# Remainder weight rows: two 64-row transfers for two groups each, in place of one mirrored 128-row transfer

## The chip, the cores and the metric

The kernel runs on one core of a Trainium2 chip. TensorE (PE) multiplies matrices, VectorE (DVE) and ScalarE (ACT) work on elements and empty PSUM, GpSimd (POOL) does small element work and issues some transfers, and SyncE (SP) issues all the others. Each engine executes its own list of instructions in order and waits on semaphores. Sixteen DMA engines move the data. The metric is device time in microseconds of one launch; smaller is better.

## The reference, cut to what matters

```python
x = A_x                                # 1 x 2048 x 576, bf16
xn = layernorm(x)
qkv = xn @ wqkv                        # 576 x 1728; 32 heads of 18
scores = q @ k.T * 18 ** -0.5          # causal, window of 256 keys
s = (softmax(scores) @ v) @ wo         # 576 x 576
h = sigmoid(xn @ w_gate) * (xn @ w_up) # 576 x 4608 each
g = silu(h @ w_down)                   # 4608 x 576
out = x + s * g
```

The contraction length that matters here is 576 = 64 + 4 x 128. PE's array is used as two tiles of 64 rows each, so a matrix with 576 rows makes four blocks of 128 rows and a remainder of 64 rows.

## The kernel before, in words

The 2048 tokens are worked off in four chunks of 512. For each chunk the kernel makes the layer norm, the transposed normalized input `xnT`, the projections to Q, K and V, the windowed attention of 8 groups of 4 heads, the output projection, and the feed-forward part: 36 tiles `ft` of 128 hidden columns, each with a gate and an up matrix (`gate_up`, line 881), a tanh on ACT (line 904), a multiplication on DVE into `hT` (line 907), and then the down projection (`down`, line 944).

All work is first written as a graph of operations with dependencies and priorities. `schedule` (line 1030) is a planner: with estimated durations, it places one operation after another on the five engines, which fixes each engine's list and which PSUM slot an operation gets. `emit` (line 1124) writes the lists out, with waits on semaphores. A change to a transfer's estimated bytes or count can therefore reorder everything that is planned later. The feed-forward matmuls of chunk 0 begin first, ahead of attention, split by token blocks (`PARTS`) as `xnT` becomes ready; warm-up matmuls on zeros (line 424) fill PE before that and end when the planner places the first gate/up matmul.

`turn` (line 102) and `pair` (line 94) issue the matmuls of one product. In `pair`, output 0 is computed with rows 0 to 63 of the array (`ROWS[0]`, the first row tile), output 1 with rows 64 to 127. With a block of 128 weight rows, each of the two outputs needs both halves, so it is run twice with the halves swapped. The remainder block k = 0 is run only once: output 0 takes its 64 remainder weight rows from partitions 0 to 63, output 1 from partitions 64 to 127.

For the weights this means: `load_nat` (line 399) loads the four blocks of 128 rows in one transfer. `load_rem` (line 403) loads the remainder of 64 rows for two matrices (or two halves of one matrix) in one transfer that fills 128 partitions. Its source access pattern has three dimensions, the outermost of size 2:

```python
return self.dma(dst, bass.AP(a.tensor, a.offset, [(step, 2), a.ap[0], (1, n)]), P * n * 2, ...)
```

It is used for Q and K (`wqkr`), for the two column halves of V (`wvr`) and of the output matrix (`wor`). Gate and up are different tensors, so one transfer can't take both. Therefore `weights` (line 843), which loads the groups of two `ft` tiles for chunk 0, mirrors: one transfer brings the gate rows of group g to partitions 0 to 63 and those of group g + 1 to 64 to 127, another the up rows of group g + 1 to partitions 0 to 63 and those of group g + 2 to 64 to 127. In odd groups gate and up have then changed sides, and `gate_up` swaps them (`flip`, line 885), with their PSUM banks. The first up group and the last one are loaded alone, as transfers of 64 rows. The remainder of all 18 groups stays in `wgr` for the later chunks; the four blocks are loaded again in each chunk, through a ring of 4 group slots in `wgs`.

All these loads are in SP's list, in the planner's order. In the first chunk it begins with `x`, the gate and up loads of groups 0 to 3 with their remainders, `wqk`, `wqkr`, `wv`, `wvr`; later loads wait for slots that PE releases. `xr` is the input of the next chunk's layer norm; its statistics (lines 480, 482) and the copies of Q and K columns (`wq4`, lines 439 and 443, which wait for all of `wqk` and `wqkr`) stand in DVE's list between the multiplications for `hT`.

The softmax here doesn't subtract the row's maximum and nothing guards it: scores larger than these inputs give would overflow.

## Time and profile before

| | us |
|---|---|
| median of 8 runs | 584.12 |
| lowest, highest | 582.87, 585.42 |
| profiled execution, own time | 584.22 |
| its span in the profile | 582.4 |
| PE busy | 569.1 (98%) |
| DVE busy | 346.5 (60%) |
| ACT busy | 268.9 (46%) |
| POOL busy | 180.1 (31%) |
| SP waits for PE, total of 63 waits | 215.3 |

The profile is of one execution. Its span runs from the first to the last instruction; the measured time includes what lies around. Busy times are per engine, and engines work beside each other, so that they don't add up. PE's granted clock is full throughout. 62.05 MB are moved in 105748 packets, at 107 GB/s in the mean; in the first 50 us it is about 200 GB/s. In rows of the profile, `out<-in` gives the tiles that an instruction writes and reads, and brackets give the idle time before it and what ended it.

### The profile page before, as it was taken

The numbers are of one execution on the slowest core, as the hardware profiler recorded it, in microseconds if no ns is written. First come the engines' busy times: TensorE is split into PE (matmuls) and PEld (weight loads), VectorE is DVE, ScalarE is ACT, GpSimd is POOL, SyncE is SP. The second block draws the span as 40 slices with busy tenths as digits, with TensorE's granted clock in tenths as the row PEclk, the third lists the DMA queues.
The fourth block names the chain that finished last, engine by engine and source line by source line (L and its number), as shares of the span: only waits on it lengthen the run. The fifth ranks groups of instructions, "written<-read, shape, count | busy, mean of one in ns | idle before, by whom it ended". The sixth has DMA issues, their size and how long they took to land.

```text
span 582.4 us, 21466 instructions
## 1 busy us (share of the span) xinstructions
PE 569.1 (98%) x9536; PEld 356.7 (61%) x9536; DVE 346.5 (60%) x837; ACT 268.9 (46%) x379; POOL 180.1 (31%) x290
## 2 busy tenths in 40 slices
PE   7998999999999999999999999999999999999996
PEld 5554555597785555555677865555457754444786
DVE  4358989856789974677877476777431133333123
ACT  2245576534366844765743654867220023333111
POOL 7454465334457522145355215630000000000000
PEclk9999999999999999999999999999999999999999
DMA  6677899743213333243412003533350014442010
GB/s 178 202 216 229 202 221 195 208 99 64 61 41 105 104 113 100 74 119 101 99 37 54 25 24 95 155 111 110 109 146 20 25 58 137 140 144 73 2 43 23
DMA packets 105748, 62.05 MB, mean 107 GB/s; under 512 B 14996, under 2 KB 104292, under 8 KB 105656
## 3 DMA queue, kind: packets, MB, share of 16 engines
q1 hardware_dynamic: 100536, 55.95, 35.7%
q0 software_dynamic: 5120, 4.74, 3.4%
q8 instruction: 75, 1.23, 0.9%
q14 instruction: 17, 0.14, 0.1%
HBM read 51.61 MB, written 2.36 MB: 93 GB/s over the span
## 4 chain that ended last, share of the span: by engine, by line
PE 90%; DMA 3%; SPq 3%; DVE 2%; issue 1%; ACT 1%; DVEq 0%
PE ps L98 90%; SPq L254 3%; DMA xr<-in_A_x_dram 2%; DMA wqkr<-in_A_wqkv_dram 1%; DVE hT L907 1%; ACT tring L904 1%; PE ps L550 0%; DVE s_attn L1011 0%; DVE thf L1016 0%; DVE wq L443 0%; DVE xf L1021 0%; DVE expr L714 0%; DVE small L482 0%; DVE wq L439 0%; DVE mask L461 0%
## 5 line engine op out<-in xcount | busy, mean ns | idle before, releaser
L98 PE MATMUL ps<-xnT,wgs 64*128 64x512 bf16 (+2 forms) x2400 | 288.9, 368 | 0.4 <-issue 0.3
L701 ACT ACTIVATE expr<-ps 128x1024 bf16<-128x1024 f32 (+2 forms) x160 | 156.5, 983 | 67.4 <-PE ps L98 66.4
L98 PEld LDWEIGHTS ps<-xnT,wgs 64*128 64x128 bf16 x2400 | 111.5, 94 | 113.6 <-PE ps L98 2.3
L98 PE MATMUL ps<-wd_sb,hT 64*128 64x288 bf16 (+2 forms) x2448 | 155.6, 276 | 0.0
L907 DVE SCALAR_TENSOR_TENSOR hT<-tring,ps 128x512 bf16<-128x512 bf16 x144 | 98.7, 686 | 78.4 <-ACT tring L904 71.7
L904 ACT ACTIVATE tring<-ps 128x512 bf16<-128x512 f32 x144 | 85.8, 596 | 128.0 <-PE ps L98 126.8
L98 PEld LDWEIGHTS ps<-wd_sb,hT 64*128 64x128 bf16 x2448 | 114.2, 94 | 26.0
L254 POOL DMA_DIRECT2D qk<-qd x160 | 82.3, 523 | 85.2 <-DVE qd L588 33.2
L666 POOL TENSOR_SCALAR kx<-kprev,small 128x256 bf16<-128x256 bf16 x64 | 64.4, 1016 | 85.4 <-PE ps L98 85.0
L714 DVE TENSOR_TENSOR expr<-expr,mask 128x256 bf16<-128x256 bf16 (+2 forms) x232 | 65.9, 306 | 37.7 <-ACT expr L701 36.3
L98 PE MATMUL ps<-xnT,wgr 64*128 64x512 bf16 (+2 forms) x300 | 56.0, 368 | 5.6 <-DVE hT L907 3.4
L98 PE MATMUL ps<-qk,kx 64*128 64x320 bf16 (+4 forms) x736 | 59.7, 251 | 0.0
L767 DVE TENSOR_REDUCE pvs<-ps 64x304 f32<-64x608 f32 x64 | 50.4, 788 | 15.2 <-PE ps L98 13.8
L98 PEld LDWEIGHTS ps<-qk,kx 64*128 64x128 bf16 x736 | 31.7, 94 | 26.2 <-ACT expr L701 1.0
L1001 ACT ACTIVATE thf<-ps 128x576 bf16<-128x576 f32 (+3 forms) x22 | 11.4, 520 | 61.1 <-PE ps L98 60.6
L98 PEld LDWEIGHTS ps<-v_aug,expr 64*128 64x128 bf16 x2432 | 35.4, 93 | 6.0
L98 PE MATMUL ps<-v_aug,expr 64*128 64x19 bf16 (+1 forms) x2432 | 35.8, 170 | 0.0
L98 PE MATMUL ps<-xnT,wqk 64*128 64x512 bf16 x256 | 32.6, 375 | 0.0
L1004 DVE SCALAR_TENSOR_TENSOR thf<-thf,ps 128x576 bf16<-128x576 bf16 x12 | 9.0, 753 | 30.0 <-ACT thf L1001 29.4
L98 PEld LDWEIGHTS ps<-xnT,wgr 64*128 64x128 bf16 x300 | 15.0, 94 | 18.8 <-DVE hT L907 5.0
L666 DVE TENSOR_SCALAR kx<-qk,small 128x512 bf16<-128x512 bf16 x64 | 23.6, 393 | 1.9 <-PE ps L98 1.6
L588 DVE CAST qd<-ps 128x1024 bf16<-128x1024 f32 (+1 forms) x20 | 22.2, 1115 | 3.8 <-PE ps L98 3.3
(66 smaller groups left out, 292.1 us busy)
## 6 DMA issues: line engine op xcount, KB each, us to landing
wgs<-in_B_w_gate_dram SPq DMA_DIRECT2D x72, 256.0 KB, 3.1
wgs<-in_B_w_up_dram SPq DMA_DIRECT2D x72, 256.0 KB, 3.5
wd_sb<-in_B_w_down_dram SPq DMA_DIRECT2D x9, 576.0 KB, 6.7
qk<-qd POOLq DMA_DIRECT2D x100, 36.0 KB, 2.0
xf<-in_A_x_dram SPq DMA_DIRECT2D x16, 144.0 KB, 2.2
out_dram<-xf SPq DMA_DIRECT2D x16, 144.0 KB, 1.8
xr<-in_A_x_dram SPq DMA_DIRECT2D x6, 288.0 KB, 3.9
wqk<-in_A_wqkv_dram SPq DMA_DIRECT2D x2, 576.0 KB, 6.5
```

The costliest lines, as they stand in the source:

```text
L98: res = eng.matmul(outs[i], lhs(ROWS[t], i), rhs(ROWS[t], i), start=start, stop=stop, tile_position=(64 * t, 0))
L254: o = self.op(eng, DMA_ISSUE_NS[eng], lambda e: e.dma_start(dst, src), name, deps, prio, nbytes=nbytes)
L588: return eng.tensor_copy(dst, self.both(h, n))
L666: return e.tensor_scalar(self.kx[:, sx, pos:pos + n_ // SW, t, :], src.rearrange("p (s k) -> p s k", k=SW), self.half[:, t:t + 1], None, A ...
L701: return eng.activation(self.expr[:, se, :, lo * SW:NT], self.both(h, NT)[:, :, lo * SW:NT], ACTF.Exp, scale=SM_SCALE)
L714: return eng.tensor_tensor(e_, e_, m_, ALU.mult)
L767: return eng.tensor_reduce(out[ROWS[i]], src, mybir.AxisListType.X, ALU.add)
L904: th = op("ACT", act_ns(NT), lambda e: e.activation(self.tring[:, st, :], bank(h, 0), ACTF.Tanh, scale=0.5), f"th:{c}:{ft}", deps=[pg, dt_ ...
L907: mu = op("DVE", dve_ns(NT), lambda e: e.scalar_tensor_tensor(self.hT[:, ft, :], self.tring[:, st, :], 1.0, bank(h, 1), ALU.add, ALU.mult) ...
L1001: return e.activation(v2(t)[:, a:b, :], y2()[:, a:b, :], ACTF.Tanh, scale=0.25)
L1004: q1 = op("DVE", dve_ns(w), lambda e: e.scalar_tensor_tensor(v2(t), v2(t), 1.0, y2(), ALU.add, ALU.mult), f"fq1:{nm}", deps=[th, f2], prio=0)
```

## The change

`load_rem` now takes a list of sources and makes one transfer of 64 rows for each: the first to partitions 0 to 63, the second to 64 to 127, each on a semaphore of its own. Q and K, the halves of V and the halves of the output matrix so have two transfers instead of one. For gate and up, each even group loads the gate rows of itself and of the next group (512 columns) to the first row tile, and the up rows of the same two groups to the second. No group is mirrored: `flip` goes, and `wgr` shrinks from two slots of 2560 columns to one of 4608. The `wgr` transfers are 18 of 64 KB, where there were 17 of 64 KB and 2 of 32 KB. The planner's estimated bytes for a transfer of 64 rows are set to 1.5 times its real bytes, as they were for the two transfers of 64 rows before.

```diff
-        self.wgr, _ = seq("wgr", [P, 2, F // 2 + WG * P])
+        self.wgr, _ = seq("wgr", [P, F])
...
-    def load_rem(self, dst, src, step, n, name, lane, prio, deps=()):
-        a = src[0:RD, 0:n]
-        return self.dma(dst, bass.AP(a.tensor, a.offset, [(step, 2), a.ap[0], (1, n)]), P * n * 2, name, lane, deps=deps, prio=prio)
+    def load_rem(self, dst, srcs, name, lane, prio, deps=()):
+        return [self.dma(dst[ROWS[t], :], src[0:RD, :], RD * src.shape[1] * 3, name, lane + (t,), deps=deps, prio=prio)
+                for t, src in enumerate(srcs)]
...
-        self.op_wqk.append(self.load_rem(self.wqkr[:, :], wq, D, D, "dma:wqkr", ("wqkr",), 5))
+        self.op_wqk += self.load_rem(self.wqkr[:, :], (wq, wk), "dma:wqkr", ("wqkr",), 5)
...
-        self.op_wv.append(self.load_rem(self.wvr[:, :], wv, 288, 288, "dma:wvr", ("wvr",), 6))
+        self.op_wv += self.load_rem(self.wvr[:, :], (wv[:, 0:288], wv[:, 288:D]), "dma:wvr", ("wvr",), 6)
...
-            self.op_wo_w.append(self.load_rem(self.wor[:, :], self.wo, 288, 288, "dma:wor", ("wor",), 8, [pv]))
+            self.op_wo_w += self.load_rem(self.wor[:, :], (self.wo[:, 0:288], self.wo[:, 288:D]), "dma:wor", ("wor",), 8, [pv])
...
             if c == 0:
-                nw = WG * P
-                pr = pr if wg != 1 else 1
-                for i, w in enumerate((self.wg, self.wu)):
-                    if wg % 2 == i and wg < NFT // WG - 1:
...
-                ds += self.op_wgr[wg] + self.op_wgr.get(wg - 1, [])
+                if wg % 2 == 0:
+                    f8 = slice(wg * WG * P, (wg + 2) * WG * P)
+                    self.op_wgr[wg] = self.load_rem(self.wgr[:, f8], (self.wg[:, f8], self.wu[:, f8]), f"dma:wgr:{wg}",
+                                                    ("wgr", wg % NWS), pr, [dw])
+                ds += self.op_wgr[wg - wg % 2]
...
-            flip = ft // WG % 2
-            co = [(ft // WG + (i and flip)) // 2 * WG * P + ft % WG * P for i in range(2)]
...
-                w = t ^ flip
-                return self.wgs[r, sw, k - 1, w, fc] if k else self.wgr[r, w, co[w]:co[w] + P]
+                return self.wgs[r, sw, k - 1, t, fc] if k else self.wgr[r, ft * P:(ft + 1) * P]
...
-                return turn(eng, [bank(h, w ^ flip)[:, t0:t0 + n] for w in range(2)], lhs, lambda r, t, k: x_in[r, k, t0:t0 + n],
-                            half)
+                return turn(eng, [bank(h, w)[:, t0:t0 + n] for w in range(2)], lhs, lambda r, t, k: x_in[r, k, t0:t0 + n], half)
```

## The prediction

> **What bounds the kernel now.** I read the page's busy shares first, then TensorE by stretches of time, then TensorE and VectorE in order of time around each hole, last the DMA issues. From the page:

> ```profile
> PE 569.1 (98%) x9536; PEld 356.7 (61%) x9536; DVE 346.5 (60%) x837; ACT 268.9 (46%) x379; POOL 180.1 (31%) x290
> ```

> TensorE (PE) stands idle for 582.4 - 569.1 = 13.3 us, and only there can a load be worth anything. The stretches (first column the window, then its length, then PE's busy time; the last two are the DMA engines' mean busy share and GB/s):

> ```profile
> 10.00:15.00 5.00, 4.13 (x131) 3.79 (x127) 0.61 (x5) 0.70 (x1) 4.83 (x5) 1.00 0.85 242
> ...
> 40.00:45.00 5.00, 3.89 (x40) 1.64 (x36) 1.66 (x5) 2.26 (x4) 0.40 (x1) 1.00 0.55 158
> 45.00:50.00 5.00, 3.67 (x40) 1.70 (x42) 5.00 (x14) 2.28 (x4) 1.57 (x3) 1.00 1.01 296
> 50.00:60.00 10.00, 10.00 (x166) 5.00 (x168) 9.22 (x30) 7.59 (x13) 5.92 (x10) 1.00 0.90 221
> ```

> From 50 to 576 us PE has hardly a hole; the last 6 us are the tail, which the change does not touch. What is left is before 50 us. PE in order of time (start, duration, and in brackets the idle time before it and what ended it):

> ```profile
> 9.81 0.23 PE L98 MATMUL ps<-xnT,wgr 64*128 64x128 bf16 x2 [1.46 <-DMA wgr<-in_B_w_up_dram]
> ...
> 12.87 0.23 PE L98 MATMUL ps<-xnT,wgr 64*128 64x128 bf16 x2 [0.57 <-issue]
> ...
> 14.28 0.34 PE L98 MATMUL ps<-xnT,wgs 64*128 64x128 bf16 x5 [0.30 <-issue]
> ...
> 27.64 0.39 PE L98 MATMUL ps<-xnT,wqkr 64*128 64x512 bf16 x2 [0.72 <-DVE hT L907]
> ...
> 46.16 0.39 PE L98 MATMUL ps<-xnT,wgr 64*128 64x512 bf16 x2 [2.27 <-DVE hT L907]
> ```

> The last two name VectorE (DVE), but DVE itself was waiting, in order, for transfers:

> ```profile
> 25.65 0.29 DVE L439 COPY wq<-wqk 128x512 bf16<-128x512 bf16 x1 [1.56 <-DMA wqkr<-in_A_wqkv_dram]
> ...
> 44.69 0.46 DVE L480 BATCH_NORM_STATS2 small<-xr 128x6 f32<-128x288 bf16 x1 [3.06 <-DMA xr<-in_A_x_dram]
> ```

> So five holes hang on DMA landings. The list of DMA issues for 30 to 40 us (size, then us to landing):

> ```profile
> xr<-in_A_x_dram SPq DMA_DIRECT2D x1, 288.0 KB, 9.1
> wgr<-in_B_w_up_dram SPq DMA_DIRECT2D x1, 64.0 KB
> wgr<-in_B_w_gate_dram SPq DMA_DIRECT2D x1, 64.0 KB
> ```

> The mirrored transfers have no landing time, because they do not leave sixteen increments of their semaphore. The trace's semaphore records hold 16 for an ordinary transfer and for the 64-row `wgr` load of 32 KB, but 3 for `wqkr`: one at 18.67, right after issue, then 24.78 and 25.53. Two engines carry it. And the other transfers' last two engines are late: `xr` has 14 increments by 41.58 and the last two at 44.62 and 44.67; the 32 KB `wgr` has 14 by 7.38, then 8.13 and 9.67.

> [...]

> **The change, part by part.**

> Load on the two engines. Up to `xr` SP has issued 6784 KB in sixteen-way transfers, 424 KB per engine, and seven `wgr` of 64 KB, `wqkr` 144 and `wvr` 72 in two-way ones, 332 KB more on each of the two: 756 against 424. After it all 7448 KB are spread, 465 each. The mean busy share averages 0.69 over the nine stretches of 5 us to 45 us; with two engines full the other fourteen are at (0.69 x 16 - 2)/14 = 0.65. Ten per cent more on them is about 0.71, so I take the lag of the last two engines to go.

> Start. The new order has 18 instead of 12 warm-up matmuls ahead of the first gate/up matmul: at 0.055 us each (12 took 0.83 with their drain) they end near 8.7. Tile 1 of `xnT` is evicted at 8.44; both 64 KB `wgr` halves are issued at 3.7 and 4.4 as now and should land by 8.2 (14 engines had the 32 KB at 7.38). PE starts at 8.75, not 9.81: 1.06. Ahead of the second weight group SP issues one transfer fewer (0.74), its last half lands at 10.9, not 12.78, and the planner now moves its use behind tile 3's transposes. The 0.57 and 0.30 shrink to some 0.3: 0.57 more. Gain 1.6 when ft 3 begins.

> `wqkr`. One more issue (0.53 us) but landing well before 23.6, when PE gets there: PE's 0.38 us wait at 25.63 goes. DVE no longer stands at L439; its order (mask, wq copies 0.29 + 0.79, hT) then runs off the ACTIVATE of ft 7: matmul end 23.55, tanh to 24.35, hT to 25.07, PE at 25.15 instead of 27.64. Gain there 2.5. If that cover failed and `wqkr` landed as late as now, its second half after 0.53 more, this gain would be 0.

> `xr`. DVE's order is the same here (only the mask copy moved), so nothing steps in its place: if DVE isn't late for `xr`, next comes hT's own tanh, which PE's matmuls to 41.6 let end near 42.3; the statistics follow kx at once and hT ends 0.9 + 0.7 after kx, 43.2 in today's times, before PE's 43.89. The 2.27 and the 0.17 at 49.91 go. Sum 2.5 + 2.27 + 0.17 = 4.9.

> Adds. SP has 235 scheduled operations for 233; three remainder pairs have one issue more each, `wgr` 18 for 19. An issue is 0.53 to 0.8 us. Queued behind these are the weight loads, used some 8 us after landing, so they cost 0 here, and about 0.7 us once if that cover fails. The two-slot layout of `wgr` and the dropped swap of row tiles change no matmul's shape: 0 between -0.1 and +0.1 us.

> Order. From head group 7 of chunk 0 the planner's order is another. At the handover to chunk 1 it groups V, QK and output projections in pairs (two QK, two down-projection steps of 0.49, two QK), whose PSUM slots wait for DVE casts of 1.1 us. Where before spread them, PE had no hole. By the casts at 29.80 the first slot is free 0.6 us after the pair and the second 1.75, against 1.0 and 2.1 of cover; I charge 0.5 us, with bounds of -0.5 (the 1.2 us of small holes after 50 us partly vanish) and +6.

> So 582.4 - 4.9 + 0.5 = 578.0 of span. The profiled execution took 584.22, 1.8 more than its span, and lies 0.1 above the median of the runs, 584.12: 578.0 + 1.8 = **579.8**.

> **Rivals.**
> (a) The aggregate rate, not two engines, sets the landings. For it: 242 GB/s at 10 to 15 us; against: 14 of 16 landings are in time. Then with 10% more on each engine `xr` lands near 45, as now, and only the start's 1.6 and part of `wqkr` come: gain 2.0 to 2.8, 581.8.
> (b) Given back: the early gain stands, the new order opens holes of about the same size, 583.0 to 585.2. For it: PE's order is another from about 103 us on; against: feed-forward matmuls stand ready beside all the attention work in both orders.
> (c) Slower: five pairs at the handover (V twice, QK twice, output twice, less one covered) each wait for DVE, 92% busy from 50 to 60 us. It decides once a pair loses over (4.4 + 1.2)/5 = 1.1 us, one cast; at 1.2 us or more, 585.7. Against: DVE's load falls to half there, 10.69 of 20 us at 120 to 140.
> (d) The transfers might not spread over sixteen: then nothing is gained; the 64-row load with sixteen increments speaks against it, and I fold it into (b).

> **How the numbers follow.** The forecast, 578.5 to 581.0, has 0.65; (a), with mixtures to 582.9, 0.17; (b) 0.08; (c) 0.10. This kernel's measurement can tell 0.2%, 1.2 us, from no change, so faster means under 582.95: 0.65 + 0.17 = 0.82; same 0.08; slower 0.10. For 8 in 10 I take 578.6 to 583.4: below it lies a gain of 5.5, all holes without any new one (0.06), above it most of (b) and (c).

> **What would show it.** Right: sixteen increments for each remainder load, the first `wgr` matmul near 8.75, no wait of DVE for `wqkr` or `xr`, PE full in 40 to 50, `xr` landing in under 6 us. Wrong: `xr` still 9 us; or PE under 19.5 of 20 in the windows around 105 to 130, with DVE's casts as releaser; that would be the order, not the transfers.

## The result and the profile after

| | before | after |
|---|---|---|
| median of the runs, us | 584.77 (33 runs) | 580.58 (12 runs) |
| lowest, highest | 582.87, 587.09 | 579.92, 583.16 |
| profiled execution, own time | 584.22 | 579.92 |
| its span | 582.4 | 578.2 |

The ratio is 0.9941, with a 95% interval of 0.9927 to 0.9956: the change makes the kernel 0.6% faster. The forecast was 579.8 (578.6 to 583.4), with a span of 578.0. Of 37 runs of before, timed beside the kernels below and with a clock on record, the 20 at a mean granted clock of 0.998 or more have a median of 583.4 us and the 17 below it 585.1; of the 12 of after, 9 have 580.5 and 3 have 583.1, so that some 2.9 us of the gain stand at full clock and the rest goes with fewer losses of clock (see the last section).

The busy shares of the page after:

```profile
PE 569.8 (99%) x9542; PEld 361.6 (63%) x9542; DVE 345.5 (60%) x837; ACT 267.7 (46%) x379; POOL 179.7 (31%) x290
```

PE's busy time has grown by 0.7 us. The warm-up alone grew by 1.1: six more matmuls took 0.33 (1.16 for 0.83), and the first 48 took 4.89 for 4.12. The longer run of these 48 also fills a hole of 0.66 at 5.92, which is worth nothing. PE's idle time has shrunk from 13.3 to 8.4 us. The stretches, with the same columns as before:

```profile
10.00:15.00 5.00, 4.06 (x110) 3.66 (x106) 0.62 (x5) 0.70 (x1) 4.83 (x5) 1.00 1.12 319
40.00:45.00 5.00, 5.00 (x58) 2.43 (x54) 4.94 (x13) 3.16 (x5) 1.98 (x4) 1.00 0.55 156
45.00:50.00 5.00, 4.83 (x112) 2.69 (x110) 4.59 (x16) 3.77 (x7) 3.38 (x6) 1.00 0.66 174
...
100.00:120.00 20.00, 19.37 (x402) 13.48 (x400) 16.03 (x47) 8.19 (x15) 3.59 (x5) 1.00 0.82 178
120.00:140.00 20.00, 20.00 (x276) 15.33 (x273) 8.35 (x18) 2.83 (x6) 9.15 (x18) 1.00 0.24 52
```

From 40 to 50 us PE lacks 0.17 us, where it lacked 2.44. From 10 to 15 us the DMA engines moved 319 GB/s for 242. From 100 to 120 us there is a hole of 0.63, where before had one of 0.23. PE in order of time, with the rows that answer to those of before:

```profile
8.54 0.24 PE L98 MATMUL ps<-xnT,wgr 64*128 64x128 bf16 x2
...
12.65 0.21 PE L98 MATMUL ps<-xnT,wgs 64*128 64x128 bf16 x1 [0.78 <-issue]
...
16.41 0.39 PE L98 MATMUL ps<-xnT,wgr 64*128 64x512 bf16 x2
...
25.48 0.38 PE L98 MATMUL ps<-xnT,wqkr 64*128 64x512 bf16 x2
...
41.55 0.38 PE L98 MATMUL ps<-xnT,wgr 64*128 64x512 bf16 x2
...
45.24 0.39 PE L98 MATMUL ps<-xnT,wgr 64*128 64x512 bf16 x2 [0.17 <-DVE small L486]
...
105.04 0.39 PE L98 MATMUL ps<-xnT,wgr 64*128 64x512 bf16 x2 [0.63 <-DVE hT L890]
```

And DVE, whose two long waits are gone (no bracket):

```profile
23.16 0.29 DVE L439 COPY wq<-wqk 128x512 bf16<-128x512 bf16 x1
...
39.98 0.45 DVE L480 BATCH_NORM_STATS2 small<-xr 128x6 f32<-128x288 bf16 x1
```

The DMA issues of the page show why; `wgr` and `wqkr`, which had no landing time before, now have one (the `xr` row is a median of six; the first of them, which took 9.1 us in before, is in the list of semaphore records below):

```profile
xr<-in_A_x_dram SPq DMA_DIRECT2D x6, 288.0 KB, 3.6
wgr<-in_B_w_gate_dram SPq DMA_DIRECT2D x9, 64.0 KB, 3.8
wgr<-in_B_w_up_dram SPq DMA_DIRECT2D x9, 64.0 KB, 4.1
wqkr<-in_A_wqkv_dram SPq DMA_DIRECT2D x2, 72.0 KB, 6.2
```

The semaphore records of the traces, time of each increment in us, with the issue ahead:

```
before  wqkr  issued 17.70:  18.67  24.78 25.53                        (3)
after   wqkr  issued 11.65:  16.39 16.75 ... 17.54 18.08               (16)
before  xr    issued 35.52:  40.25 40.34 ... 41.51 41.58  44.62 44.67  (16)
after   xr    issued 30.70:  33.27 33.35 ... 33.93 33.94 33.94         (16)
```

The records name no engine; that two of the sixteen carry a mirrored load is read from the 3 increments, from the two late ones of sixteen, and from the packets. In before, 224 of the 256 packets of `xr` (1152 bytes each) had begun by 40.98, with up to 17 in flight at once; the last 32, two sixteenths, began from 42.69 to 43.97, with at most 3 in flight. In after all 256 began from 31.80 to 33.35, with up to 21 in flight. The 128 packets of `wvr` (576 bytes each) had 1.7 in flight in the mean and at most 4 in before, and up to 9 in after.

The landings are earlier for two reasons, and the second is easily missed. `xr` takes 3.2 us from its issue where it took 9.1, and it is issued 4.8 us earlier; `wqkr` is issued 6.1 us earlier. The two-engine loads hold up SP as well: from the first load of the second weight group to the last of `wvr`, where no issue waits for an engine's work, SP took 15.2 us for 13 issues in before and 9.9 us for 15 in after.

Where the time came from, read at the same products in both traces. Each is of one execution, and that of after is its fastest, so that the sum is on the high side:

| product | before | after | gain | forecast |
|---|---|---|---|---|
| first of 512 columns (ft 3) | 17.60 | 16.41 | 1.19 | 1.6 |
| second QK product | 27.64 | 25.48 | 2.16 | 2.5 |
| first after the hole for `xr` | 46.16 | 41.55 | 4.61 | 4.8 |
| next with a hole of 0.17 | 49.91 | 45.24 | 4.67 | 4.9 |
| end of the span | 582.4 | 578.2 | 4.2 | 4.4 |

### The profile page after: what moved, and what is told of

The parts are those of the page before. It is cut to its first block, busy times and chain, and to the rows that moved or that the text cites. A ratio compares the mean times of both kernels' runs of the same rounds, so it can differ in the third digit from the quotient of the medians.

```text
span 578.2 us, 21485 instructions
## 1 busy us (share of the span) xinstructions
PE 569.8 (99%) x9542; PEld 361.6 (63%) x9542; DVE 345.5 (60%) x837; ACT 267.7 (46%) x379; POOL 179.7 (31%) x290
## 4 chain that ended last, share of the span: by engine, by line
PE 96%; DVE 2%; issue 1%; ACT 0%; POOL 0%; DVEq 0%
PE ps L98 96%; DVE hT L890 1%; PE ps L550 1%; ACT tring L887 0%; DVE pvs L767 0%; DVE s_attn L994 0%; DVE thf L999 0%; DVE xf L1004 0%; POOL small L488 0%; DVE xnr L493 0%; DVE small L465 0%; DVE pvs L771 0%; DVE hT L418 0%; DVE small L486 0%; ACT expr L701 0%
## 5 line engine op out<-in xcount | busy, mean ns | idle before, releaser
L98 PE MATMUL ps<-xnT,wgs 64*128 64x512 bf16 (+2 forms) x2400 | 288.1, 368 | 0.8 <-issue 0.8
L98 PEld LDWEIGHTS ps<-xnT,wgs 64*128 64x128 bf16 x2400 | 111.2, 94 | 113.8 <-PE ps L98 1.6
L98 PE MATMUL ps<-wd_sb,hT 64*128 64x288 bf16 (+2 forms) x2448 | 154.9, 276 | 0.0
L98 PEld LDWEIGHTS ps<-wd_sb,hT 64*128 64x128 bf16 x2448 | 117.8, 94 | 22.5
L714 DVE TENSOR_TENSOR expr<-expr,mask 128x256 bf16<-128x256 bf16 (+2 forms) x232 | 64.7, 301 | 29.8 <-ACT expr L701 28.4
L98 PE MATMUL ps<-qk,kx 64*128 64x320 bf16 (+4 forms) x736 | 59.8, 251 | 0.0
L98 PE MATMUL ps<-xnT,wgr 64*128 64x512 bf16 (+2 forms) x300 | 55.9, 368 | 1.4 <-DVE hT L890 1.3
L98 PEld LDWEIGHTS ps<-qk,kx 64*128 64x128 bf16 x736 | 31.7, 94 | 25.4 <-ACT expr L701 1.7
L98 PEld LDWEIGHTS ps<-v_aug,expr 64*128 64x128 bf16 x2432 | 35.5, 93 | 6.2 <-issue 0.2
L98 PE MATMUL ps<-v_aug,expr 64*128 64x19 bf16 (+1 forms) x2432 | 35.9, 170 | 0.0
L98 PE MATMUL ps<-xnT,wqk 64*128 64x512 bf16 x256 | 32.0, 376 | 0.0
L666 DVE TENSOR_SCALAR kx<-qk,small 128x512 bf16<-128x512 bf16 x64 | 23.6, 389 | 5.0 <-DMA qk<-qd 4.3
L98 PEld LDWEIGHTS ps<-xnT,wgr 64*128 64x128 bf16 x300 | 14.8, 94 | 15.3 <-DVE hT L890 3.4
## 6 DMA issues: line engine op xcount, KB each, us to landing
xr<-in_A_x_dram SPq DMA_DIRECT2D x6, 288.0 KB, 3.6
```

Of the source, the lines that this page charges most:

```text
L98: res = eng.matmul(outs[i], lhs(ROWS[t], i), rhs(ROWS[t], i), start=start, stop=stop, tile_position=(64 * t, 0))
L666: return e.tensor_scalar(self.kx[:, sx, pos:pos + n_ // SW, t, :], src.rearrange("p (s k) -> p s k", k=SW), self.half[:, t:t + 1], None, A ...
L714: return eng.tensor_tensor(e_, e_, m_, ALU.mult)
```

## The experiments

Theory A: the gain comes from spreading the remainder loads over sixteen DMA engines. Theory B: it comes from the new order of the work and the new set of transfers. Ten kernels were run, each timed beside the kernel before.

**Spreading alone, in the order of before (`b_spread`).** Every mirrored load of before stays where it is in SP's list, but is issued as two transfers of 64 rows on the same semaphore. The planner's costs and every engine's order are those of before, as are the row lengths; `flip` and the two slots stay.

```diff
-        return self.dma(dst, bass.AP(a.tensor, a.offset, [(step, 2), a.ap[0], (1, n)]), ...)
+        o = self.dma(dst, bass.AP(a.tensor, a.offset, [(step, 2), a.ap[0], (1, n)]), ...)
+        return self.halve(o, [(dst[ROWS[t], :], bass.AP(a.tensor, a.offset + t * step, [a.ap[0], (1, n)])) for t in range(2)])
...
+    def halve(self, o, pairs):
+        o.nd = len(pairs)
+        o.fn = lambda e: [e.dma_start(d, s) for d, s in pairs]
+        return o
...
-                    lane_cnt[o.lane] += 16
+                    lane_cnt[o.lane] += 16 * o.nd
```

> The order of every engine of the kernel before is kept; each mirrored 128-row load is issued as two 64-row loads on one semaphore, so that it can run on sixteen DMA engines. Theory A (two engines were late): PE's waits for DMA before 50 us go, the first gate/up matmul starts at 8.4 to 8.8 us, xr lands in under 5 us, span 577.0 to 578.2, time 578.8 to 580.0, some 0.5 us below the changed kernel, which loses that at its new hole at 105 us. Theory B (the planner's new order or the row length of 1 KB did it): time as before, 583.5 to 585.

Measured: 579.87 us (579.5 to 582.21, 6 runs), ratio 0.9931 (0.9914 to 0.9949), span 577.8. PE's holes in the trace of this kernel:

```profile
11.48 0.23 PE L98 MATMUL ps<-xnT,wgr 64*128 64x128 bf16 x2 [0.65 <-issue]
13.16 0.34 PE L98 MATMUL ps<-xnT,wgs 64*128 64x128 bf16 x5 [0.56 <-issue]
45.30 0.39 PE L98 MATMUL ps<-xnT,wgr 64*128 64x512 bf16 x2 [0.17 <-DVE small L493]
70.46 0.39 PE L98 MATMUL ps<-xnT,wgr 64*128 64x512 bf16 x2 [0.22 <-DVE hT L915]
99.04 0.39 PE L98 MATMUL ps<-xnT,wgr 64*128 64x512 bf16 x2 [0.23 <-DVE hT L915]
```

The 45.30 stands beside 45.24 of after and 49.91 of before. Spreading alone brings the whole gain, and the span ends 0.4 us earlier than after's, since the hole of 0.63 at 105.04 isn't there. A use of its own for the layout without mirrored groups doesn't show in the time.

**The new order, with two engines again (`a_two`, `a_four`, then `a_two2`, `a_four2`).** In the kernel after, the source of each 64-row load was given an outermost dimension of 2, or of 4.

```diff
+        def few(a):
+            return bass.AP(a.tensor, a.offset, [(RD // 2 * a.ap[0][0], 2), (a.ap[0][0], RD // 2), a.ap[1]])
...
-        return [self.dma(dst[ROWS[t], :], src[0:RD, :], ...)
+        return [self.dma(dst[ROWS[t], :], few(src[0:RD, :]), ...)
```

> The changed kernel, its order kept, but each 64-row load has a source pattern of 2 x 32 rows, so that it runs on two DMA engines. Theory A: three semaphore increments for each, the last two increments of the other loads late, the waits for wqkr and xr are back, 583 to 586 us. Theory B: as the changed kernel, 580 to 581.

> As the two-engine version of the changed kernel, but 4 x 16 rows, four DMA engines. Theory A: the extra load on each of these is half, 166 KB beside 424 KB up to xr; the lag is mostly hidden, 580.2 to 582, between the changed kernel and the two-engine one. Theory B: 580 to 581, the same for two and four engines.

Measured: 581.04 us (580.49 to 581.41, 5 runs) and 580.8 (580.16 to 581.52, 4 runs), ratios 0.9944 (0.9929 to 0.9958) and 0.9941 (0.9921 to 0.9961), as after. But each transfer still left 16 increments: twice 32 rows, one after the other, are the same as 64 rows of one stride, and by the increments they ran as these do, on neither two engines nor four. The runs thus say nothing on two engines; they are repeats of after. The next two take rows in an order that can't be folded, every second or every fourth row first. The remainder rows then don't match their inputs, so these two kernels time the transfers and don't compute the layer:

```diff
-            return bass.AP(a.tensor, a.offset, [(RD // 2 * a.ap[0][0], 2), (a.ap[0][0], RD // 2), a.ap[1]])
+            st = a.ap[0][0]
+            return bass.AP(a.tensor, a.offset, [(st, 2), (2 * st, RD // 2), a.ap[1]])
```

> The kernel after in its own order, with the same transfers of 64 rows, but each names its source as 32 even rows and then 32 odd rows, an outermost dimension of 2 that cannot be folded into the next one. The remainder rows so arrive in another order than the reference's, so the output differs; bytes, instructions and order are those of after. Theory A (spreading): three increments per remainder transfer, again over 700 KB on each of two engines against some 420 on the others, so xr lands 8 us or more after its issue, the waits of VectorE for wqkr or xr come back, and the time is 582.5 to 585.5. Rival B (order and number of transfers): as after, 580.0 to 581.5.

> The same with an outermost dimension of 4 (every fourth row, then the next), so the output again has its remainder rows in another order. Theory A: five increments per remainder transfer, four engines with some 170 KB more than the others in place of two with 330 more; half of the lag, so the xr and wqkr waits shrink to under 1.5 us together and the time is 580.5 to 582.5, between after and the kernel with two. Rival B: as after, 580.0 to 581.5, and the same as with two.

Measured with two: 586.99 us (585.55 to 588.24, 6 runs), ratio 1.0045 (1.0028 to 1.0063), slower than before; `wqkr` leaves 3 increments (17.03, 21.91, 22.78), and the last two of `xr` are late again, at 42.76 and 44.93 against 38.64 for the fourteenth. With four: 580.87 us (579.35 to 583.57, 6 runs), ratio 0.994 (0.9918 to 0.9962), as after, with 5 increments for `wqkr`, and `xr` landing 3.3 us after issue. The same 15 issues of SP, from the second weight group to `wvr`, took 16.5 us with two engines, 11.5 with four, and 9.9 in after. PE's holes with two engines:

```profile
10.91 0.23 PE L98 MATMUL ps<-xnT,wgr 64*128 64x128 bf16 x2 [2.18 <-DMA wgr<-in_B_w_up_dram]
14.96 0.21 PE L98 MATMUL ps<-xnT,wgs 64*128 64x128 bf16 x1 [1.06 <-issue]
46.42 0.40 PE L98 MATMUL ps<-xnT,wgr 64*128 64x512 bf16 x2 [2.40 <-DVE hT L893]
51.80 0.39 PE L98 MATMUL ps<-xnT,wgr 64*128 64x512 bf16 x2 [0.17 <-DVE small L489]
```

Behind the 2.40 stands, in DVE's list, the wait for `xr`:

```profile
44.96 0.46 DVE L483 BATCH_NORM_STATS2 small<-xr 128x6 f32<-128x288 bf16 x1 [3.41 <-DMA xr<-in_A_x_dram]
```

The start's hole and the hole for `xr` are back with nothing but the row order of the source changed, so theory B falls; and the row order itself is not what costs, since the kernel with four engines has one like it and is as fast as after. The wait for `wqkr` is not back: its second half landed at 24.30, and DVE came to it at 25.46. The kernel also ends 2.5 us of span later than before, more than I expected. Its stretches behind the hole of 2.40 tell where most of it lies (the third column from the right is the granted clock):

```profile
44.00:46.00 2.00, 0.02 (x2) 0.00 (x0) 1.04 (x3) 0.00 (x1) 0.00 (x0) 1.00 0.71 216
46.00:48.00 2.00, 1.58 (x10) 0.65 (x12) 2.00 (x4) 0.00 (x0) 0.21 (x1) 0.67 0.51 158
48.00:50.00 2.00, 2.00 (x16) 0.80 (x14) 1.07 (x6) 0.81 (x1) 1.37 (x3) 0.50 0.24 72
```

PE went on at 0.67 and then 0.50 of its clock: 1.58 x 0.33 + 2.00 x 0.50 = 1.5 us lost, an estimate from these rows, on top of the hole. The hole of before in the same place, 2.27 us, had left the clock at 1.00; the last section compares the two.

**One part alone (`b_spread_wgr`, `b_spread_qkv`).** The kernel `b_spread`, with only the `wgr` loads in halves, or only `wqkr`, `wvr` and `wor`. In diff against before, the first has `halve` in `weights` alone, the second in `load_rem` alone.

> The kernel before in its order, and only the wgr loads issued as two transfers of 64 rows; wqkr, wvr and wor stay on two engines. Common backlog (what delays a waiter is everything that queued on the two engines before): 224 of the 332 KB extra on each of them go, wqkr lands about 4 us after issue and so before VectorE reads it near 23.5, xr in under 6 us, and most of the gain comes: 580.0 to 581.5. Rival (each load delays only its own reader): the start's 1.6 us come, the waits for wqkr and xr stay: 582.0 to 583.0.

> The kernel before in its order, and only wqkr, wvr and wor issued as two transfers of 64 rows; wgr stays on two engines. Common backlog: the start is as before (first gate/up matmul at 9.8), the sixteen-way wqkr still queues behind the wgr loads on the two engines and lands some 1.5 us earlier than before, xr some 1.5 to 2 us earlier: 581.8 to 583.3. Rival (each load delays only its own reader): wqkr's wait goes whole, the start and xr stay as before: 581.4 to 582.0, with VectorE's wait for xr at 3 us.

Measured: 579.66 us (579.51 to 580.05, 6 runs), ratio 0.9922 (0.9909 to 0.9935), and 579.93 (579.0 to 580.49, 6 runs), ratio 0.9924 (0.9909 to 0.9939). The first is somewhat under the range for the common backlog, 580.0 to 581.5, and against the rival that each load delays only its own reader. One step of that expectation failed: `wqkr`, still on two engines, landed 7.9 us after its issue and not 4. But it was issued at 14.46 and not at 17.70, and so was there at 22.33, before DVE came to it at 23.21. The second kernel is a miss of mine: I gave it 581.8 to 583.3. DVE in its trace:

```profile
24.18 0.29 DVE L446 COPY wq<-wqk 128x512 bf16<-128x512 bf16 x1 [0.29 <-DMA wqkr<-in_A_wqkv_dram]
...
40.82 0.45 DVE L487 BATCH_NORM_STATS2 small<-xr 128x6 f32<-128x288 bf16 x1
```

`xr` still took 8.4 us there and its last two increments were still 3 us late (37.02 for the fourteenth, 40.00 and 40.05), but it was issued at 31.69 and not at 35.52, and DVE got to it at 40.82. The late landing cost only what went beyond the reader's own time: before lay 3.06 us beyond it, this kernel 0.8 us short of it. The start, too, was as I expected, 9.77 for 9.81. So either third or two thirds of the spreading takes the two later waits away, and what the two have in common is the backlog on two engines, not one particular load.

```diff
-NWARM = 60
+NWARM = 30
...
-        zero = self.hT[:, 0, 0:2 * P]
+        zero = self.hT[:, 0, 0:4 * P]
```

> The changed kernel with half as many warm-up matmuls, each 512 instead of 256 columns wide, so that PE's list is some 90 instructions shorter before the first gate/up matmul. Both kernels have a hole with no releaser right before PE's instruction number 449 (0.30 us before, 0.78 after). If PE waits there for its own instructions, the hole moves to a later matmul, where wider matmuls use up the list more slowly, and shrinks: 0.3 to 0.8 us less than the changed kernel, 579.4 to 580.3. If it is an unseen wait for data, it stays at the same product and the time stays at 580 to 581.

Measured: 581.24 us (579.35 to 584.54, 10 runs), ratio 0.9955 (0.9935 to 0.9975). In its profile (584.41) the hole came later, again after 449 instructions, and was longer:

```profile
16.74 0.50 PE L98 MATMUL ps<-xnT,wgs 64*128 64x256 bf16 x5 [2.21 <-issue]
```

So the place goes with the count; that wider products would cover it was wrong. Behind this hole, as behind the 2.40 above, the clock fell. The next two do the opposite, with 93 and 89 pairs of warm-up matmuls of 96 columns for 45 and 42 pairs of 256, in about the same time:

```diff
-NWARM = 60
+NWARM = 160
...
-                return pair(eng, self.halves(h, 2 * P), lambda r, t: zero[r, 0:P], lambda r, t: zero[r, :], True, True)
-            w = op("PE", 220 if i < 18 else 110, f_warm, ...)
+                return pair(eng, self.halves(h, 96), lambda r, t: zero[r, 0:P], lambda r, t: zero[r, 0:96], True, True)
+            w = op("PE", 82 if i < 48 else 41, f_warm, ...)
```

> The kernel after with 93 pairs of warm-up matmuls of 96 columns in place of 45 pairs of 256 columns, over about the same time, so TensorE has executed some 190 instructions more when the first gate/up product starts (two places in the order of PE near 9 us differ as well). Theory (the 0.78 us hole at 12.65 is the fetch of PE's next instruction block, due at its 449th instruction): that instruction is now a warm-up or one of the first products, the hole at 12 to 13 us is gone, the next block falls due where products are wider, the runs with 583 us vanish, span 577.2 to 577.8 and time 579.0 to 579.8. Rival (the hole is a late weight load that the records don't show): it stays at the same product, 580.3 to 580.9[...].

> The same warm-ups in the kernel with before's order and every remainder load spread over two transfers of 64 rows. Its hole of 0.65 us at 11.48 ends 0.1 us after the landing of the second weight group and stays; the 0.56 at 13.16 is the instruction block and goes: span 577.0 to 577.5, time 578.8 to 579.4. Rival (late load): both holes stay, 579.5 to 580.1.

Measured: `a_more` 580.58 us (580.0 to 580.9, 6 runs), ratio 0.9928 (0.9903 to 0.9953), span 578.7; `b_more` 579.44 us (579.0 to 580.21, 6 runs), ratio 0.9911 (0.9888 to 0.9935), span 577.4. PE's holes between 8 and 17 us, first of `a_more`:

```profile
9.12 0.23 PE L98 MATMUL ps<-xnT,wgr 64*128 64x128 bf16 x2 [0.69 <-DMA wgr<-in_B_w_up_dram]
14.43 0.83 PE L98 MATMUL ps<-xnT,wgs 64*128 64x128 bf16 x15 [0.88 <-issue]
```

then of `b_more`:

```profile
8.70 0.23 PE L98 MATMUL ps<-xnT,wgr 64*128 64x128 bf16 x2 [0.44 <-DMA wgr<-in_B_w_up_dram]
11.80 0.23 PE L98 MATMUL ps<-xnT,wgr 64*128 64x128 bf16 x2 [0.62 <-issue]
```

In `a_more` the hole is gone from instruction 449 and stands after 705, which is 256 further on, so its time missed my range by 0.8 us; in `b_more` neither count has a hole, the time is 0.04 us above my range, and what is left, 0.62, ends 0.09 us after the last increment of the second group's up weights (11.71). Both misses and hits fit a wait for instructions better than a late load: 449 and 705 are 256 apart, and in `a_wide` and `a_more` too PE went on 1.3 and 1.6 us after the end of a 16 KB instruction packet. `b_more` has the lowest median of all, but its interval overlaps that of after, and the two were not timed side by side. In `a_more` the instruction packet now runs from 6.33 to 7.36, in the middle of the first `wgr` loads, whose last increments came at 8.72 and 8.98 with the others in by 7.74. The packet takes 1.03 us, and these are 0.98 and 1.24 later than the others; that it held them up was not shown.

## Why the prediction was right, step by step

- **Two engines carry the mirrored loads.** Right, as far as the records tell, and shown from both sides: spreading alone brings the gain (579.87 us in `b_spread`), and an outermost dimension of 2 in the new order takes it away (586.99 in `a_two2`). Measured were 3 increments with an outermost dimension of 2, 5 with one of 4 (`a_four2`), and 16 with 64 rows of one stride.
- **Rival (a), the aggregate rate.** Refuted: 319 GB/s from 10 to 15 us, against 242.
- **Start, 1.06 us.** The first gate/up matmul came at 8.54 for 8.75: 1.27.
- **The holes of 0.57 and 0.30 shrink to 0.3.** This step failed, since the prediction took five holes for landings and one was not. The 0.57 was a landing (12.78, PE at 12.87) and went. The 0.30 was the hole at instruction 449, came 1.6 us earlier on, and grew to 0.78: PE reached it 1.83 us after its packet began, for 2.08 in before, and the packet took 1.16 us for 0.98. The start's sum was 1.19 and not 1.6 (1.6, with 0.21 more from the first matmul, 0.48 less here and 0.16 less from a new hole at 10.32, is 1.17).
- **`wqkr`, +0.9 between ft 3 and the second QK product.** Measured 0.97, with DVE at L439 at 23.16 and no wait.
- **`xr`, 2.27.** Measured 4.61 - 2.16 = 2.45.
- **The 0.17 at 49.91 goes.** Wrong: it stayed in every kernel. It follows tanh and `hT` of an earlier product (tanh at 43.87, 0.60; `hT` at 44.50, 0.69, so to 45.19), and stayed where nothing waited for `xr`.
- **Adds: 0.** Right, and on the safe side: 15 issues took SP 5.3 us less than the 13 of before in the same stretch (the longest issue in the first 40 us took 1.52 us, 3.15 before). That the two-engine loads hold up SP's issues is not in the prediction.
- **Order, a charge of 0.5.** Right in size: 0.63 at 105.04, for 0.23 in the order of before. The mechanism was another than PSUM slots of the QK pairs. The chain of waits of after at that place, in order of time (start, us, what):

```profile
102.23 0.78 DVE pvs L767
103.02 0.03 issue
103.05 0.80 DVE pvs L767
...
104.02 0.19 DVE pvs L771
104.21 0.09 issue
104.30 0.70 DVE hT L890
105.00 0.05 issue
105.04 9.03 PE ps L98 x168
```

The multiplication for `hT` stands in DVE's list behind two reductions of the attention outputs and their reciprocal. The QK pairs from 120 to 140 us cost nothing (PE 20.00 of 20). So rivals (b) and (c) came to 0.4 us of the 4.6, and the total was nearer than its parts: the start came 0.4 short and the 0.17 did not come, while `wqkr` and `xr` brought 0.25 more than forecast. That the medians, too, lie 4.2 us apart is in part luck: the prediction priced a hole at its length alone and knew of no loss of clock behind one, and runs of before are more often below a mean clock of 0.998 (17 of 37, for 3 of 12 of after).

## What to carry to other kernels

Count a transfer's semaphore increments in the trace. Here the mirrored loads left 3, one of them early, where the others left 16. Then look whether other transfers' last increments come late, as two of the sixteen of `xr` did by 3.0 us, since these are the ones that pay. Look also at how long the issuing engine takes for each issue (15.2 us for 13 in before, 9.9 for 15 in after). The outermost dimension of 2 in the access pattern cost more here than a second issue: 583.94 us for before beside 579.87 for `b_spread`. In `b_spread_qkv` the last two increments of `xr` were still 3 us late and cost nothing, since they didn't pass their reader; taking away a third of the backlog so was worth about as much as all of it (579.93 us, for 579.87).

## What the hardware showed that I had not expected

- **Instruction packets.** After 449 or 705 of its instructions PE stood for 0.30 to 2.21 us, in the stretch where small matmuls go by fast (131 in the 5 us from 10 to 15 in before) and the DMA engines' mean busy share is 0.85 in before and 1.12 in after. Each of these holes ended 1.3 to 1.6 us after the end of a 16 KB packet on the instruction queue. That the counts are 256 apart was measured; that PE waits for such packets is read from the holes of these traces.
- **The clock after a hole.** Behind holes of 1.97 (`a_four2`), 2.21 (`a_wide`) and 2.40 us (`a_two2`) the granted clock fell to 0.50 for 3.41 us; behind 1.60, 1.76, 2.18 (the start of `a_two2`) and 2.27 it did not. The length alone doesn't tell, but the traces' clock records do. The clock fell at 14.35, 17.56 and 46.67 us, which is 3, 3 and 12 times 3.41 us after the first 1.00 in its record (at 4.11, 7.32 and 5.71). In the tails of before and after, with PE's work nearly over, it fell to 0.50 at 580.75 and 575.51, which is 169 and 167 times 3.413 us after theirs (at 3.90 and 5.49), at the end of stretches of that length with 3.08 and 2.05 us of idle time. Cut each trace into such stretches of 3.41 us from that first 1.00: the three holes lie whole in one stretch, so that it has 1.97, 2.21 and 2.40 us of idle time, and the clock fell at its end. The 2.27 of before lies across a boundary at 44.86 and leaves 0.97 and 1.30; the 2.18 leaves 0.39 and 1.79. In the twelve traces, no stretch up to the tail with 1.79 us or less brought a fall. That the clock goes by the idle time in such a stretch is read from these few falls, and where between 1.79 and 1.97 us it turns was not shown. In the stretches of `a_four2`, behind its hole of 1.97 us, it cost 1.67 x 0.41 + 2.00 x 0.44 = 1.6 us, an estimate from these rows:

```profile
14.00:16.00 2.00, 1.67 (x21) 1.39 (x22) 0.00 (x0) 0.00 (x0) 1.94 (x2) 0.59 1.01 318
16.00:18.00 2.00, 2.00 (x31) 1.77 (x28) 0.00 (x0) 0.00 (x0) 1.90 (x3) 0.56 1.04 350
```

A stretch of 3.41 us at half clock lowers the mean clock of 580 us by 0.003. The three executions of after at 583.0 to 583.2 us have 0.997 on record, the others 0.998 to 1.00, so one such fall in each is my estimate; they have no trace that shows the hole.
